# First products of a token pair from three experts instead of two, and a store moved from ScalarE's queue to SyncE's, in a chunked-scan and expert-merge kernel

## Chip, cores and metric

The kernel runs on one core of a Trainium2 chip. The metric is the device time of one execution in microseconds (us), the median of several runs. TensorE is the engine for matmuls (PE in the profile), VectorE is DVE, ScalarE is ACT, GpSimd is POOL, SyncE is SP.

## What is computed

Two parts follow each other. The first is a chunked state-space scan (Mamba-2 style) over 4 sequences, 8 heads, 768 positions, head size 32, state size 16. The second sends each of the 4 x 768 = 3072 tokens, now 256 wide, through 4 experts with 1024 hidden features each and adds the results by the token's domain probabilities:

```python
for c in range(nc):                      # chunks of a sequence
    L = np.exp(cum[:, :, :, None] - cum[:, :, None, :]) * causal
    y_intra = ((C @ B^T) * L) @ x        # inside the chunk
    y_inter = (C @ state) * np.exp(cum)  # from the chunks before
    state = decay_full * state + sum over j of (B x) * decay_from_j
...
p = domain_probs / (domain_probs.sum(-1, keepdims=True) + 1e-09)
for e in range(4):
    out += p[:, e:e+1] * (np.maximum(x @ w1[e], 0.0) @ w2[e])
```

All arithmetic is float32.

## The kernel before

**Tokens and weights.** Positions are worked on in 24 chunks of 128 tokens; two chunks make a pair of 256 tokens. The pairs are grouped into five blocks (`ORDER`, line 327): three blocks of two pairs (scheme `B`) and two of three pairs (scheme `H`). The experts' features are cut into 16 feature blocks `fb` of 256, four per expert (`EPB`, line 363). For a feature block `w1` and `w2` are 256 KB each.

**Products with sums.** The matmuls with `w1` and `w2` are not taken one by one: scheme `B` takes two feature blocks (a "two") and two pairs together and needs 7 products in place of 8, scheme `H` takes three and three and needs 15. Most products work on sums of weight halves (line 957) and sums of token halves (`token_sums`, lines 966 to 980, buffers `Y`). A product is two matmul instructions in the code (`product`, line 862, recorded at line 866) and four in the profile. In scheme `B` the products numbered 1 and 2 need neither kind of sum and only the first pair's tokens. `twos_begun` (line 1006) takes these two for one two: product 1, a copy of the bank by ScalarE (`snap`, line 873, recorded at 875), product 2 into the same bank, and then the gate: VectorE applies the ReLU and the probability (`gated`, line 898, recorded at 901). The rest of the two follows later in `twos_first` (line 1015), where ScalarE puts the copy back into a bank (`seed`, line 878, recorded at 880). The products with `w2` are gathered by `second` (line 1150); each `house` of results is copied out by ScalarE (1143, 1146).

**Scan side.** For a chunk, `fetch` (line 736) loads tokens (`xb`), decays spread over partitions (`ab`, line 434, from the stored table `acut_d`) and from the fifth chunk on the decays by head (`ah`, line 440, from the stored table `ac_d`). `decays` (line 750) has VectorE's scans (`LT`, line 490; `dec`, line 772), a small product on GpSimd (500) and ScalarE's masks (`ctm`, line 466). `scores` (line 779) is a matmul (473) and four masks on VectorE (`MT`, line 790); `outputs` (line 798) the matmuls that give the tokens (506, 812) and their copies by ScalarE (827, 516).

**Order.** Lines 383 to 692 are written in order by hand and treat the first two chunks. Line 691 stores the probabilities (`p_d`, from which the gate tables `gate` are loaded at line 854), line 692 stores `ac_d` by a DMA that ScalarE issues. Everything after is recorded as `Work` and ordered by `Plan.run` (line 182): it carries a clock for each engine with estimated costs, TensorE's order is fixed by the list `line`, and every other engine takes the ready work with the earliest due time. `KEEP` (used at 163) holds buffers back from work that is not urgent; `NEAR`, `WORTH` and `FIRST` (lines 232 to 237) let VectorE wait briefly for work that is more urgent than what is ready. So constants and TensorE's order decide the order on VectorE, ScalarE, GpSimd and in SyncE's queue, in which nearly all DMAs are issued. DMAs share eight completion counters, so an issue also waits until the DMA that had its counter eight places before has landed.

**The part at issue.** Lines 1286 to 1310 begin the planned part: four twos (feature blocks 0 to 7, two experts) get operands and `twos_begun`; their eight first products are put around `scores([2, 3])` and `outputs([2, 3])` (five ahead of the scores, `SCORED`, three behind), and then come the four products with `w2` that need nothing else (`second(0, ..., [(1, 2)])`). The loop from line 1340 goes through the units: for the first block unit 0 has feature blocks 0 to 3, unit 1 has 4 to 7 and so on. Lines 1344 and 1345 load a unit's weights one unit ahead. `EARLY` gives the units in which stored sums for scheme `H` are prepared, and `PAIRS_AT` the places in a unit's product list where the next block's chunks have their scores (`s`) and outputs (`o`).

Of the kernel before, what the change touches and what calls it, by code (L numbers as in the profile page):

```python
# [18 lines left out]
HOP = 0.06  # L19
D512, D256 = .60, .34  # L20
LANDING = 2.2
KEEP = 5
NV, NW = 33, 28
SLACK, BACK, YIELD = 0.0, 3.0, 0.0
EARLY = 3, 4, 5, 5, 6, 7, 8, 9, 10, 11
SOFT = 1
ROUND = 0, 3, 2, 0, 4
RATE, MARGIN = 330.0, 2.0
AFTER = 1
HOLD = 6.0  # L30
NEAR, WORTH, FIRST = .3, 3.0, 25.0
WAIT = .15
LANES, ISSUE = 8, .48
URGENT = {}
SCORED = 5
EASY = 40.0
HELD = ("x", "w"), (5, 8), (0, 7)
APART = (0, 7),
# [2 lines left out]
LATE = (13, 2), (6, 9), (11, 4), (10, 12), (3,), (1, 14), ("x", "w"), (5, 8), (0, 7)  # L41

PAIRS_AT = {
    (0, 2): ((1, 12, "s0"), (2, 5, "s1"), (2, 22, "o01")),
    (4, 2): ((0, 1, "s0"), (2, 1, "s1"), (2, 14, "o01")),
    (4, 3): ((0, 1, "s0"), (0, 14, "o0"), (1, 1, "s1"), (2, 1, "s2"), (2, 14, "o12")),
    (6, 3): ((0, 1, "s0"), (0, 14, "o0"), (2, 1, "s1"), (3, 1, "s2"), (3, 14, "o12")),
# [28 lines left out]
class Plan:  # L76
# [65 lines left out]
    def homed(self, w, at):  # L142

        taken, when = {}, at
        for v in w.touched:
# [14 lines left out]
            if v.kind == "bank" and len(self.spare["bank"]) <= sum(  # L160
                    x.home is None and x.place < v.place for x in self.banks):
                return None, None
            if v.kind == "V" and len(spare) <= KEEP and w.latest + self.late > at + 8:
                return None, None
# [172 lines left out]
def kernel(  # L337
# [10 lines left out]
    nc = tc.nc  # L348

    NCH, _, W = xbc.shape  # L350
# [12 lines left out]
    EPB = F // FB  # L363
# [24 lines left out]
    ac_d = tc.dram_tile([NCH, NH, P], FP32, name="ac_d")  # L388
# [137 lines left out]
    a_sb, a_cut = (homes["V"][-4][:NCH * NH // 2, i].rearrange("p (r s) -> p r s", r=2) for i in range(2))  # L526
# [62 lines left out]
    def store_decays(engine, d, sb):  # L589
        engine.dma_start(  # L590
            out=d.rearrange("c h s -> (c h) s").rearrange("(p r) s -> p r s", r=2), in_=sb)
# [97 lines left out]
        keep_state(1, A[1][:, t], y[:, P:])  # L689
    mask(2, ctm[0], xb[2])  # L690
    nc.sync.dma_start(out=p_d.rearrange("e c s -> c e s"), in_=p_sb)
    store_decays(nc.scalar, ac_d, a_sb)

# [1 line left out]
    line = []  # L697
# [308 lines left out]
    def twos_begun(k, fbs):  # L1006

        seq = []
        mul = opener(k, fbs, seq)
        b1 = mul(1)  # L1010
        s1 = snap(b1)
        mul(2, b1)
        return seq, s1, gated(b1, gate_of(k, fbs[0]), 0)
# [103 lines left out]
    def visit(k, house, terms, last=False, only=None):  # L1117

        seq = []
        terms = [t for t in terms if only in (None, t[0])]  # L1120
        held = kept.get((k, house))
        both = len({t[0] for t in terms}) == 2 or held is not None and held.both
        lo, to = 0, FB * (2 if both else 1)
        if only is not None:
            lo, to = FB * house.index(only), FB * house.index(only) + FB
        bank = seed(held, lo, to) if held is not None else value("bank", fills=both)
        begun = held is not None
        for which, w, view, x in terms:
            half = house.index(which)
            seq.append(plan.add({"PE": .863}, lambda e, half=half, view=view, x=x, begun=begun: product(  # L1130
                bank.t, half, view(), x.t, not begun), reads=[w, x], writes=[bank]))
            begun = True
        bank.both = both
        if last:
            kept[k, house if only is None else (only,)] = bank
            return seq
        v = kept[k, house] = value("V")
        v.both = both or len(house) == 2
        if not both and len(house) == 2:
            plan.add({"POOL": .4}, lambda e: nc.gpsimd.memset(  # L1140
                v.t[:, 1 - house.index(terms[0][0])], 0.0), part=[v])
        if both:
            act(.5, lambda e: nc.scalar.copy(out=flat(v), in_=bank.t), reads=[bank], writes=[v])  # L1143
        else:
            lo = FB * house.index(terms[0][0])
            act(.3, lambda e: nc.scalar.copy(  # L1146
                out=flat(v)[:, lo:lo + FB], in_=bank.t[:, lo:lo + FB]), reads=[bank], writes=[v])
        return seq

    def second(k, groups, houses, held=(), more=()):  # L1150

        seq = []
        for house in houses:
            terms = [
                (r, weights[k, fbs, 2][0][r][0], lambda r=r, fbs=fbs: weights[k, fbs, 2][1](r), T[r])
                for r in house for fbs, T in groups if r in T]
            terms += [t for t in more if t[0] in house]
            for only in reversed(house) if house in held and house in APART else (None,):
                if terms:
                    seq += visit(k, house, terms, house in held, only)  # L1160
        return seq
# [9 lines left out]
    def plain_terms(k, fbs, h, parts):  # L1171
        return [(blocks[k].scheme.plain[d, n], weights[k, fb, 2],
                 lambda fb=fb, d=d: w2_half(weights[k, fb, 2].t, d), h[fb, n])
                for d, n in parts for fb in fbs]
# [103 lines left out]
    def put(*seqs):  # L1278

        n = [len(s) for s in seqs]  # L1280
        keys = [((i + (.5 if len(seqs) == 1 else (j + .5) / len(seqs))) / n[j], j, i)
                for j, s in enumerate(seqs) for i in range(n[j])]
        return [seqs[j][i] for _, j, i in sorted(keys)]
# [3 lines left out]
    for l, at in ((1, 0), (2, 1)):  # L1287
        for i, fb in enumerate(range(0, 8 // l, 2)):
            loaded[fb, l] = plan.taken("W", fb + at, now + 1.0 + 0.6 * i)
    twos = [(fb, fb + 1) for fb in range(0, 8, 2)]  # L1290

    st[2]["a"] = [value("bank", fills=False) for _ in range(NQ)]
    fetch(3)
# [4 lines left out]
    for i in range(2):  # L1298
        tokens[0, i + 1] = yT[0, 0], lambda v, i=i: v.t[:, i]
    begun = {two: twos_begun(0, two) for two in twos}  # L1300
    firsts = [begun[twos[x + i]][0][j] for x in (0, 2) for j in range(2) for i in range(2)]
    decays(2)
    decays(3)
    line.extend(firsts[:SCORED])
    scores([2, 3])
    line.extend(firsts[SCORED:])
    outputs([2, 3])
    line.extend(second(0, [(two, {1: h}) for two, (_, _, h) in begun.items()], [(1, 2)]))
    for c in range(4):
        carry(c)  # L1310
    units, last_made = [], {}
# [28 lines left out]
    for u, (k, groups) in enumerate(units):  # L1340
        b = blocks[k]
        of_block = [v for v, (q, _) in enumerate(units) if q == k]
        i = u - of_block[0]
        if 1 < u + 1 < len(units):
            unit_weights(*units[u + 1])
        if i == 0 and k:
            token_sums(k)
        if groups is None:
            gates.pop((k, 0), None)
            seq, h = [], {}  # L1350
            for n in range(b.scheme.pairs):
                s, h[0, n] = plain_first(k, 0, n)
                seq += s
            plain = plain_terms(k, [0], h, b.scheme.plain)
        else:
            made = [threes_first(k, fbs) if b.scheme is H else twos_first(
                k, fbs, begun.get(fbs) if k == 0 else None) for fbs in groups]
            seq = put(*[s for s, _ in made])
            right = twos_right if b.scheme is B else threes_right
        merged = put(behind, seq) if behind else seq  # L1360
        ends.append(merged[-1])
        if ending is not None:
            leave(*ending, due=lambda n=u + AFTER: ends[min(n, len(ends) - 1)])
            ending = None
        for _ in range(EARLY.count(u)):
            operands("early", H, *early.pop(0), merged[0],
                     lambda n=u + SOFT: ends[min(n, len(ends) - 1)])
        if groups is None:
            behind = second(k, *held, HELD if k == len(blocks) - 1 else (), plain)
        else:  # L1370
            held = [(fbs, right(h)) for fbs, (_, h) in zip(groups, made)], b.scheme.houses
            for fbs, T in held[0]:
                if k == 0 and fbs in begun:
                    del T[1]
            plain_next = u + 1 < len(units) and units[u + 1][1] is None
            if plain_next:
                held = held[0], LATE
            behind = [] if plain_next else second(k, *held)
        if u == of_block[-1] and k < len(blocks) - 1:
            ending = k, result(k)  # L1380

        at = {}
        if k < len(blocks) - 1:
            for unit, x, what in PAIRS_AT[len(of_block) if k else 0, blocks[k + 1].scheme.pairs]:
                if unit != i:
                    continue
                cs = [blocks[k + 1].first + 2 * int(p) + j for p in what[1:] for j in range(2)]
                mark = len(line)
                if what[0] == "s":
                    for c in cs:  # L1390
                        fetch(c)
                        decays(c)
                    scores(cs)
                else:
                    outputs(cs)
                    for c in cs:
                        carry(c)
                at[x] = line[mark:]
                del line[mark:]
        for x, w in enumerate(merged):  # L1400
            line.extend(at.get(x, []))
            line.append(w)
# [54 lines left out]
```

## Time and profile before

| What | Value |
| --- | --- |
| time, median of 3 runs | 627.83 us (627.7, 627.83, 630.71) |
| the profiled execution's own time | 629.19 us |
| its span, first to last instruction | 627.2 us |
| granted TensorE clock in it | 0.998 of full speed |
| matmuls of line 866: instructions, busy | 2640, 428.4 + 211.7 us by tile |
| weight, token and table traffic | 127.45 MB, 203 GB/s in the mean |

The busy time of engines in stretches, and the share of time in which the DMA engines were busy:

| us | PE | DVE | ACT | POOL | DMA share | GB/s |
| --- | --- | --- | --- | --- | --- | --- |
| 0 to 10 | 10.00 | 7.37 | 4.09 | 6.57 | 0.61 | 190 |
| 10 to 20 | 8.26 | 6.24 | 5.09 | 1.51 | 0.76 | 261 |
| 20 to 30 | 9.95 | 10.00 | 6.13 | 0.42 | 0.95 | 317 |
| 30 to 40 | 8.83 | 10.00 | 4.65 | 0.56 | 1.03 | 381 |
| 40 to 50 | 10.00 | 9.85 | 4.59 | 3.10 | 0.82 | 258 |
| 50 to 60 | 10.00 | 8.72 | 2.73 | 6.58 | 1.00 | 323 |
| 60 to 80 | 20.00 | 20.00 | 8.29 | 12.55 | 0.72 | 242 |
| 80 to 100 | 20.00 | 19.85 | 12.27 | 11.41 | 0.76 | 252 |
| 100 to 150 | 50.00 | 47.15 | 19.34 | 22.16 | 0.64 | 211 |
| 150 to 627 | 471.43 | 390.49 | 207.40 | 98.47 | 0.59 | 188 |

In the profile's rows a tile's buffer number is left out: `bank` is an accumulation bank, `v` a token or result buffer, `w` a weight buffer, `Y` a sum of tokens. A row of the timeline gives start, length, engine, line, operation, what is written and read, the number of merged instructions, and in brackets the idle time of the engine before it and what ended that. ACTq and SPq are the queues of ScalarE and SyncE at a DMA issue. In a list of waits the numbers are total time, times, and the longest.

### The profile page before, as it was taken

How to read it: one execution, taken by the hardware profiler on the slowest of the kernel's cores; microseconds unless marked ns; L12 is line 12 of the kernel's file. 1: busy time of each engine (PE TensorE's matmuls, PEld its weight loads, DVE VectorE, ACT ScalarE, POOL GpSimd, SP SyncE). 2: the span in 40 equal slices, each digit the busy share in tenths (PEclk: the TensorE clock that was granted, in tenths of full speed). 3: DMA queues.
4: the chain of work that ended last, by engine and by line, in shares of the span. 5: the costliest groups of instructions: out<-in, count | busy, mean ns of one | idle time of the engine just before them, and what ended most of it. 6: DMA issues, size and time to landing. Idle time of an engine off the chain costs nothing.

```text
span 627.2 us, 10263 instructions
## 1 busy us (share of the span) xinstructions
PE 617.3 (98%) x3427; PEld 525.9 (84%) x3427; DVE 529.6 (84%) x886; ACT 274.6 (44%) x580; POOL 163.3 (26%) x201
## 2 busy tenths in 40 slices
PE   8999999999999999999999999999999999999997
PEld 4778888888888888888788888888888888888886
DVE  7899999996878798869689989959786977869684
ACT  4533463433355344235534345445444335454441
POOL 4016656630385664333441000100020000000000
PEclk9999999999999999999999999999999999999999
DMA  7798768663699978389999737636222329743001
GB/s 251 263 357 302 237 206 286 212 206 108 210 353 372 301 236 299 98 261 345 336 357 299 242 71 249 194 96 200 61 93 68 82 50 299 225 142 110 1 1 51
DMA packets 112629, 127.45 MB, mean 203 GB/s; under 512 B 28981, under 2 KB 78145, under 8 KB 112577
## 3 DMA queue, kind: packets, MB, share of 16 engines
q1 hardware_dynamic: 112308, 126.64, 62.1%
q8 instruction: 27, 0.44, 0.3%
q14 instruction: 26, 0.20, 0.1%
q10 hardware_dynamic: 268, 0.16, 0.1%
HBM read 101.87 MB, written 24.89 MB: 202 GB/s over the span
## 4 chain that ended last, share of the span: by engine, by line
PE 83%; DVE 8%; DMA 3%; SPq 3%; issue 2%; ACT 1%; POOL 0%; ACTq 0%; DVEq 0%; POOLq 0%
PE bank L866 79%; DVE v L893 3%; SPq L1250 2%; DMA w<-in_w_dram 2%; DVE v L901 2%; PE bank L506 1%; PE bank L473 1%; DMA xb<-in_xbc_dram 1%; DVE w L957 1%; DVE MT L790 1%; DVE LT L490 1%; PE bank L812 1%; DVE v L1195 0%; ACT v L875 0%; ACT A L516 0%
## 5 line engine op out<-in xcount | busy, mean ns | idle before, releaser
L866 PE MATMUL bank<-v,w 128*128 128x256 f32 x1816 | 428.4, 380 | 2.0 <-ACT v L875 1.7
L866 PEld LDWEIGHTS bank<-v,w 128*128 128x128 f32 x1816 | 343.1, 190 | 53.9 <-issue 2.8
L866 PE MATMUL bank<-Y,w 128*128 128x256 f32 x824 | 211.7, 380 | 2.9 <-ACT v L875 1.3
L893 DVE TENSOR_TENSOR v<-v,v 128x512 f32<-128x512 f32 x269 | 188.8, 735 | 26.1 <-ACT v L875 24.7
L866 PEld LDWEIGHTS bank<-Y,w 128*128 128x128 f32 x824 | 155.6, 190 | 27.5 <-ACT v L875 2.7
L880 ACT COPY bank<-v 128x512 f32<-128x512 f32 (+1 forms) x200 | 112.2, 571 | 81.1 <-DVE v L893 47.0
L901 DVE SCALAR_TENSOR_TENSOR v<-bank,gate 128x512 f32<-128x512 f32 x172 | 116.6, 683 | 31.6 <-PE bank L866 26.9
L875 ACT COPY v<-bank 128x512 f32<-128x512 f32 x112 | 65.3, 584 | 101.5 <-PE bank L866 101.2
L957 POOL TENSOR_TENSOR w<-w,w 128x256 f32<-128x256 f32 x105 | 91.6, 894 | 40.2 <-PE bank L866 18.4
L1143 ACT COPY v<-bank 128x512 f32<-128x512 f32 x105 | 61.4, 584 | 90.4 <-PE bank L866 88.0
L893 POOL TENSOR_TENSOR v<-v,v 128x512 f32<-128x512 f32 x11 | 18.4, 1669 | 281.4 <-DVE v L893 142.6
L490 DVE TENSOR_TENSOR_SCAN LT<-ab,ident 128x512 f32<-128x512 f32 x42 | 53.4, 1290 | 2.1 <-DMA ab<-acut_d 2.1
L893 DVE TENSOR_TENSOR v<-bank,v 128x512 f32<-128x512 f32 x40 | 27.4, 685 | 6.7 <-PE bank L866 6.2
L790 DVE TENSOR_TENSOR MT<-bank,LT 128x512 f32<-128x512 f32 x44 | 27.3, 680 | 1.2 <-PE bank L473 1.2
L1195 DVE TENSOR_TENSOR v<-v,v 128x256 f32<-128x256 f32 x54 | 21.8, 437 | 7.7 <-ACT v L1143 7.6
L500 POOL TENSOR_TENSOR MT<-xb,LT 128x64 f32<-128x64 f32 (+1 forms) x28 | 14.2, 514 | 48.5 <-DVE LT L490 25.6
L957 POOL TENSOR_TENSOR w<-w 128x256 f32<-128x256 f32 x14 | 16.1, 1155 | 37.4 <-DMA w<-in_w_dram 18.9
L1146 ACT COPY v<-bank 128x256 f32<-128x256 f32 x23 | 8.6, 372 | 35.7 <-PE bank L866 35.5
L775 POOL TENSOR_TENSOR cts<-ctm,dec 128x256 f32<-128x256 f32 x20 | 16.2, 816 | 26.7 <-ACT ctm L466 19.7
L466 ACT ACTIVATE ctm<-xb,tmask 128x128 f32<-128x128 f32 x48 | 16.5, 396 | 13.3 <-DMA xb<-in_xbc_dram 11.9
L1042 DVE TENSOR_TENSOR bank<-bank,v 128x512 f32<-128x512 f32 x24 | 16.4, 687 | 3.5 <-PE bank L866 3.5
L957 DVE TENSOR_TENSOR w<-w,w 128x256 f32<-128x256 f32 x33 | 15.4, 503 | 0.0
(72 smaller groups left out, 204.5 us busy)
## 6 DMA issues: line engine op xcount, KB each, us to landing
w<-w_d SPq DMA_DIRECT2D x138, 256.0 KB
w<-in_w_dram SPq DMA_DIRECT2D x126, 256.0 KB
w_d<-w SPq DMA_DIRECT2D x82, 256.0 KB
ab<-acut_d SPq DMA_DIRECT2D x21, 512.0 KB
w<-in_w_dram SPq DMA_DIRECT2D x42, 128.0 KB
gate<-p_d SPq DMA_DIRECT2D x10, 384.0 KB
xb<-in_xbc_dram SPq DMA_DIRECT2D x17, 192.0 KB
gate<-p_d SPq DMA_DIRECT2D x11, 256.0 KB
```

Source lines behind the costliest of these rows:

```text
L466: nc.scalar.mul(ctm[:, t], xb[:, OCT:OCT + P], tmask[:, t:t + 1])
L490: nc.vector.tensor_tensor_scan(out=LT.rearrange("p h s -> p (h s)")[:, lo:lo + w], data0=src, data1=ident.rearrange("p h s -> p (h s)")[:, ...
L790: nc.vector.tensor_mul(s["MT"].t[:, js, h, 0:P], g, s["LT"].t[:, js, h])
L866: nc.tensor.matmul(out=o, lhsT=w[:, j], rhs=x if half is None else x[:, j], start=(start and j == 0), stop=(j == 1), skip_group_check=True)
L875: act(.5, lambda e: nc.scalar.copy(out=flat(v), in_=bank.t), reads=[bank], writes=[v])
L880: act(.54 if to - lo > FB else .32, lambda e: nc.scalar.copy(out=bank.t[:, lo:to], in_=flat(v)[:, lo:to]), reads=[v], writes=[bank])
L893: plan.add(engines, lambda e: (on(e).tensor_add if sign > 0 else on(e).tensor_sub)(flat(v), whole(x), whole(y)), reads=[x, y], writes=[v], ...
L901: dve(D512, lambda e: nc.vector.scalar_tensor_tensor(out=h.t, in0=whole(x).rearrange("p (j m) -> p j m", j=JJ), scalar=0.0, in1=g.t[:, 2 * ...
L957: plan.add({"POOL": .72} if due else B256, lambda e, r=r, x=x, y=y, sign=sign: (on(e).tensor_add if sign > 0 else on(e).tensor_sub)(view(r ...
L1042: dve(D512, lambda e: nc.vector.tensor_sub(b5.t, b5.t, flat(t)), reads=[t], writes=[b5])
L1143: act(.5, lambda e: nc.scalar.copy(out=flat(v), in_=bank.t), reads=[bank], writes=[v])
L1195: plan.add(engines, lambda e: (on(e).tensor_add if sign > 0 else on(e).tensor_sub)(o[1](), x[1](), y[1]()), reads=[v for v in vs if v is n ...
```

## The change

It takes the first products of the first pair ahead for six twos (feature blocks 0 to 11, three experts, `AHEAD`) instead of four. The four added first products stand behind `outputs([2, 3])`, two added products with `w2` follow with the others, and units 0, 1 and 2 of the first block no longer load their weights a unit ahead, since they are all named at the start. The store of `ac_d` goes into SyncE's queue. The numbers that steer the plan change too: `KEEP`, `WORTH`, `SCORED`, `EARLY` and the places of the second block's chunks. `MIXED` is false, so its branch is not taken; in the last hunk two pieces of scan work at the same place would both be kept.

```diff
-KEEP = 5
+KEEP = 4
-EARLY = 3, 4, 5, 5, 6, 7, 8, 9, 10, 11
+EARLY = 2, 3, 4, 5, 6, 7, 8, 9, 10, 11
-NEAR, WORTH, FIRST = .3, 3.0, 25.0
+NEAR, WORTH, FIRST = .3, 1.0, 25.0
-SCORED = 5
+SCORED = 4
+AHEAD = 3
+MIXED = False
...
-    (0, 2): ((1, 12, "s0"), (2, 5, "s1"), (2, 22, "o01")),
+    (0, 2): ((1, 9, "s0"), (2, 1, "s1"), (2, 18, "o01")),
...
-    store_decays(nc.scalar, ac_d, a_sb)
+    store_decays(nc.sync, ac_d, a_sb)
...
-    twos = [(fb, fb + 1) for fb in range(0, 8, 2)]
+    twos = [(fb, fb + 1) for fb in range(0, AHEAD * EPB, 2)]
...
-    firsts = [begun[twos[x + i]][0][j] for x in (0, 2) for j in range(2) for i in range(2)]
+    firsts = [begun[twos[x + i]][0][j] for x in range(0, len(twos), 2) for j in range(2) for i in range(2)]
...
     line.extend(firsts[:SCORED])
     scores([2, 3])
-    line.extend(firsts[SCORED:])
+    line.extend(firsts[SCORED:8])
     outputs([2, 3])
-    line.extend(second(0, [(two, {1: h}) for two, (_, _, h) in begun.items()], [(1, 2)]))
+    line.extend(put(firsts[8:], second(0, [(two, {1: begun[two][2]}) for two in twos], [(1, 2)])) if MIXED else [
+        *firsts[8:], *second(0, [(two, {1: begun[two][2]}) for two in twos], [(1, 2)])])
...
-        if 1 < u + 1 < len(units):
+        if AHEAD <= u + 1 < len(units):
             unit_weights(*units[u + 1])
...
-                at[x] = line[mark:]
+                at.setdefault(x, []).extend(line[mark:])
```

## The prediction

> **What bounds the kernel now.** I read the engine rows of the page first:
>
> ```profile
> PE 617.3 (98%) x3427; PEld 525.9 (84%) x3427; DVE 529.6 (84%) x886; ACT 274.6 (44%) x580; POOL 163.3 (26%) x201
> ```
>
> TensorE (PE) is busy 617.3 of 627.2 us, so only its waits can be won. The Trainium skill (Trainium Kernel Development and Optimization, Performance Expectations) says that matmul busy time is a bad measure of the distance to the limit, and that the busy share of the weight loads is a good one. By that rule 16% of the span, 100 us, would be open. The rows speak against it here: where nothing waits, x4 matmuls of L866 (one product) start every 0.86 us (45.54, 46.41, 47.27 in the timeline), 216 ns apiece, whatever the weight loads leave free. The change keeps the number of products, so I count only what exceeds 216 ns a matmul. The waits of TensorE in the first 60 us come next (total, times, longest):
>
> ```profile
> PE bank L866 <- ACT v L875: 1.7, 1, 1.7
> PE bank L866 <- ACT bank L880: 0.9, 1, 0.9
> PE bank L866 <- DVE v L901: 0.2, 1, 0.2
> ```
>
> Over the whole span the list adds 1.3 us for L875 and 0.7 us for L790; these lie near 309, 378 and 406 us. The timeline of TensorE (start, length, what, idle before) places the early ones:
>
> ```profile
> 12.68 1.99 PE L866 MATMUL bank<-v,w 128*128 128x256 f32 x8
> 16.42 2.86 PE L866 MATMUL bank<-v,w 128*128 128x256 f32 x12 [1.75 <-ACT v L875]
> ...
> 24.75 3.72 PE L866 MATMUL bank<-v,w 128*128 128x256 f32 x16
> 28.31 5.93 PE L866 MATMUL bank<-Y,w 128*128 128x256 f32 x24
> 35.10 2.33 PE L866 MATMUL bank<-Y,w 128*128 128x256 f32 x8 [0.86 <-ACT bank L880]
> 37.67 2.86 PE L866 MATMUL bank<-v,w 128*128 128x256 f32 x12 [0.24 <-DVE v L901]
> ```
>
> From row to row I subtract count x 0.216: 16.42 - 12.68 - 1.73 = 2.01 us lost; 35.10 - 28.31 - 5.18 = 1.61; 37.67 - 35.10 - 1.73 = 0.84. Together 4.5 us; all else before 60 us loses 0.1 to 0.3 at changes of shape. The first loss is explained by the timelines of ScalarE, VectorE and SyncE's queue:
>
> ```profile
> 13.16 0.69 ACT L466 ACTIVATE ctm<-xb,tmask 128x128 f32<-128x128 f32 x2
> 14.76 0.35 ACTq L590 DMA_DIRECT2D ac_d<-v  x1
> 15.21 0.69 ACT L466 ACTIVATE ctm<-xb,tmask 128x128 f32<-128x128 f32 x2 [1.36 <-DMA w<-in_w_dram]
> 15.81 1.05 ACT L875 COPY v<-bank 128x512 f32<-128x512 f32 x2
> ```
>
> ```profile
> 13.30 2.39 DVE L490 TENSOR_TENSOR_SCAN LT<-bank,ident 128x256 f32<-128x256 f32 x4
> 17.67 0.69 DVE L901 SCALAR_TENSOR_TENSOR v<-bank,gate 128x512 f32<-128x512 f32 x1 [1.98 <-PE bank L866]
> 18.28 2.33 DVE L490 TENSOR_TENSOR_SCAN LT<-ab,ident 128x512 f32<-128x512 f32 x2
> ```
>
> ```profile
> 12.17 0.51 SPq L448 DMA_DIRECT2D w<-in_w_dram  x1
> 16.51 0.34 SPq L854 DMA_DIRECT2D gate<-p_d  x1
> 16.90 0.43 SPq L448 DMA_DIRECT2D w<-in_w_dram  x1
> ```
>
> ScalarE stands at its DMA issue (L590) until a weight load lands; the masks of chunk 3 and the first copies (L875) queue behind it, and TensorE waits for a copy. SyncE issues nothing from 12.68 to 16.51. VectorE idles until 17.67 and is then full until 49 us, where the losses at 35 and 37 lie.
>
> **The store on SyncE's queue.** It leaves ScalarE (0.35 us of issue, and the wait before it) and joins SyncE's queue behind L691. A rule of the Trainium skill (same page, Key Constraints) speaks against a gain: queues share the DMA engines, and issuing from several engines only saves sequencer time. By the rule the move is worth ScalarE's 0.35 us and costs SyncE as much. By the row the issue also holds ScalarE from 13.76 (13.16 plus 0.60, the spacing of 15.21 and 15.81) to 15.21: 1.45 us. I take the row. Chunk 3's tokens must have landed: issued at 7.70, and the weight load issued at 8.88 landed 5.86 us later in the chain view, so by the same delay 13.6; at the latest with that load, 14.73. So masks 13.76, copies 14.36 to 14.94, TensorE again at 14.98: 1.44 us won; at the late bound 0.5. On SyncE 96 KB and one issue (about 0.35 us) come ahead of one weight load, inside the empty stretch 12.68 to 16.51, which hides them; without it 0.35 us on every later load.
>
> **Six products moved forward.** The two twos of the third expert bring four first products (two each) and two second ones: 6 x 0.864 = 5.18 us of TensorE go from unit 2 to before unit 0. The built order has 1722 TensorE instructions in both kernels, so nothing is added. SCORED 4 puts the scores one product earlier, which swaps neighbours. Walk of TensorE after: four products to 16.71 (12.68 + 3.46 + 0.57 of wait), scores 1.08 to 17.8, four products to 21.24. VectorE now scans chunk 3 when its decays have landed, not after the gate of the first product: at the latest 16.5, when SyncE's L854 had seen the younger transfer of L691. 16.5 + 2.33 + 2.48 (four masks L790) = 21.3, so outputs run 21.3 to 22.9 instead of 23.15. Next the four new products: their second halves wait for two L875 copies, which stand behind the copies of the outputs and four L516 pieces each on ScalarE (24.39 to 26.5 before, 1.9 earlier now): the last starts at 25.8 where TensorE is ready at 25.5. Loss 0.3 to 0.4 plus 0.1 to start again. Six second products then end at 31.8, where the first product with sums starts. Before it was 28.31; 28.31 + 5.18 = 33.5, so 1.7 us are won by there.
>
> **Weights behind them.** Unit 2's two loads of w1 and two of w2 (1 MB) and a gate table (256 KB) now go ahead of the operands of unit 0's sums. 1.25 MB at 317 GB/s (windows row 20 to 30 us, DMA share 0.95) is 4 us; SyncE's empty stretch takes one load that before left at 16.90. So sums' operands land some 3.3 us later, and TensorE asks for them 3.5 us later: hidden, with little to spare. VectorE's two more gates (0.6 each) come earlier, not anew.
>
> **The losses at 35 and 37.** They came from gates (L901) behind weight sums on VectorE, with each bank refilled only after its gate. In the new order the next product refills another bank, so the loss at 35 goes. But VectorE's order now puts a scan half (1.2 us, L490) between two gates of unit 0; a product waits for the second: 38.7 + 1.2 + 0.6 = 40.5 against 39.7, so 0.8 us stay late, and the gate before adds 0.1. The small waits between 28 and 34 (1.61 less 0.86 and its restart, some 0.6) follow the same alternation of two banks, and I keep 0.5.
>
> **Sum.** Lost before 4.5. Lost after: 0.57 and 0.1 at 14.4; 0.45 at 25; 0.5 in the sums' products; 0.9 to 1.1 at 38 to 40: 2.6. Won 1.9; VectorE says the same another way: full from 17.67, it starts its backlog 1.2 to 1.6 us earlier. Further on (KEEP, EARLY, WORTH, the places of the pairs) the order changes until about row 315 of TensorE's 1722 and is then the same; no loss shows there before. VectorE's last 364 instructions and ScalarE's last 234 keep their order, so I keep the losses at 378 and 406. At 309 ScalarE's mask waits for tokens; one mask now stands three copies earlier in that order, worth between -0.8 and +1.4 us; the nearest row is the old wait, so 0. I take 2.0 won. The profiled execution took 629.19 for a span of 627.2; it would take 627.2, and the median, 1.36 below that execution, goes from 627.83 to 625.8.
>
> **Rivals.**
> - All waits close: the scan does not fall between the gates, and the wait at 309 goes. 1.9 + 1.0 + 1.3 = 4.2 won: 623.6. For it: the list of waits has no other entry of weight. Against: the built order of VectorE shows the scan there.
> - VectorE is the limit from 20 to 49 us (10.00, 10.00 and 9.85 busy in the windows), and its two early gates and one more combine (TensorE's first sums wait in its line) eat the start: 0.5 won, 627.3.
> - Slower, by the DMA engines: they are full from 20 to 60 us (share 0.95, 1.03, 0.82, 1.00), and 12.8 MB go through in 40 us there (317, 381, 258, 323 GB/s). All later operands now follow 1.25 MB more. The first sum of unit 2 comes at 53.4 us when I carry the walk on, its load lands near 46.5: 7 us of slack. If the stretch runs at 258 GB/s throughout, 12.8 MB take 9.6 us more: 2.6 us late, VectorE stands at that sum in order with the gates behind it and TensorE behind the gates: 2.0 won less 2.6, 628.4. At the 242 GB/s of the row 60 to 80 it is 12.9 us, 5.9 late, 631.7. It decides from about 245 GB/s down. Against: the same transfers, mostly in the same sizes, made 320 in the mean, and the row at 40 to 50 has a share of only 0.82, so it is not the engines' limit.
> - The store moves but ScalarE then waits for tokens until 14.73: 0.9 less, 626.7, inside the likeliest range.
>
> **Chances.** Likeliest case 0.50 (625.8, own range 624.7 to 627.0), all waits close 0.24, VectorE 0.13, slower 0.13. Within 0.5% (3.1 us, about what a measurement of this kernel can tell from no change) lie the likeliest and VectorE: 0.62 after a little of the likeliest goes faster; faster 0.25, slower 0.13. The range 623.4 to 629.3 takes in the 258 GB/s of the slower case, leaves out the rest of it and the far edge of the best: under 2 in 10.
>
> **What would show it.** The copies L875 start near 14.4 and TensorE's row near 15.0; no ACTq row for ac_d; the first product with Y near 31.8; its 0.86 wait on L880 gone, a wait on L901 near 39; VectorE idle for under 1 us near 16. A wait of TensorE on DVE w L957 or of VectorE on DMA w in 22 to 32 us would show the slower rival; a new wait past 80 us would make the sum wrong.

## The result and the profile after

| | before | after |
| --- | --- | --- |
| median of 20 runs each | 628.44 us | 626.26 us |
| ratio after to before, 95% interval | | 0.9963 [0.9948, 0.9977] |
| the profiled execution, its span | 629.19, 627.2 us | 626.43, 624.6 us |
| granted clock in it | 0.998 | 1.000 |

One of the 20 runs after was disturbed (2292.82 us) and is left out of the ratio. The change wins 2.2 us by the medians, 0.37%. The forecast said 2.0 us and "within 0.5%", and both hold. The two profiles differ by 2.6 us of span, 0.4 us more than the medians, so a part of what follows belongs to these two executions and not to the change. How that sum comes about differs from the forecast, and the traces and four experiments show where.

The first part of the page after gives the engines' busy time:

```profile
PE 617.5 (99%) x3427; PEld 525.4 (84%) x3427; DVE 534.4 (86%) x888; ACT 273.5 (44%) x580; POOL 170.5 (27%) x199
```

TensorE has the same 3427 instructions and the same busy time (617.5 for 617.3). What has gone is waiting. Line numbers after are two or three higher: products 868, copies 877, seeds 882, gates 903, masks of the scores 792, scan 492, ScalarE's masks 468, the store 592.

The timeline of TensorE after, over the stretch shown of before:

```profile
12.49 1.99 PE L868 MATMUL bank<-v,w 128*128 128x256 f32 x8
14.84 1.99 PE L868 MATMUL bank<-v,w 128*128 128x256 f32 x8 [0.36 <-ACT v L877]
...
17.84 3.80 PE L868 MATMUL bank<-v,w 128*128 128x256 f32 x16
21.80 1.69 PE L508 MATMUL bank<-MT,xb 128*32 128x144 f32 x32 [0.15 <-DVE MT L792]
23.41 3.06 PE L868 MATMUL bank<-v,w 128*128 128x256 f32 x12
26.71 6.31 PE L868 MATMUL bank<-v,w 128*128 128x256 f32 x28 [0.24 <-ACT v L877]
32.86 7.55 PE L868 MATMUL bank<-Y,w 128*128 128x256 f32 x32
40.40 1.13 PE L868 MATMUL bank<-v,w 128*128 128x256 f32 x4
42.11 1.99 PE L868 MATMUL bank<-v,w 128*128 128x256 f32 x8 [0.58 <-DVE v L903]
```

Read it as before: start to start, less 216 ns a matmul. 14.84 - 12.49 - 1.73 = 0.62 lost at the first copies (2.01 before). 21.80 - 17.84 - 3.46 = 0.50 ahead of the outputs (0.27 before, at 20.29). 26.71 - 23.41 - 2.59 = 0.71 at the added products. 0.10 up to 32.86, then 0.63 in the sums' products to 40.40, then 42.11 - 40.40 - 0.86 = 0.85 at a gate. Together 3.4 us. Before, by the same count, the three losses make 4.5 and the two changes of shape (0.27, and 0.10 at 24.75) another 0.4: 4.8 us. That is 1.4 us won, and the first product starts 0.19 earlier in this profile. Matmul by matmul, the kernel after leads by 1.54 us at 112 us, which fits.

ScalarE's timeline shows the cure at its root:

```profile
12.96 1.36 ACT L468 ACTIVATE ctm<-xb,tmask 128x128 f32<-128x128 f32 x4
14.23 1.04 ACT L877 COPY v<-bank 128x512 f32<-128x512 f32 x2
```

All four masks run in one piece and the copies follow at once. No ACTq row stands between. The store is now in SyncE's queue:

```profile
12.43 0.51 SPq L592 DMA_DIRECT2D ac_d<-v  x1
12.99 0.98 SPq L450 DMA_DIRECT2D w<-in_w_dram  x2
17.39 0.34 SPq L856 DMA_DIRECT2D gate<-p_d  x1
```

It takes 0.51 us of a queue that issues nothing from 13.97 to 17.39. VectorE's timeline has the two places where the forecast was to be tested (the second part is from around 40 us):

```profile
17.32 2.34 DVE L492 TENSOR_TENSOR_SCAN LT<-ab,ident 128x512 f32<-128x512 f32 x2 [1.82 <-DMA ab<-acut_d]
19.77 2.48 DVE L792 TENSOR_TENSOR MT<-bank,LT 128x512 f32<-128x512 f32 x4
...
39.06 1.28 DVE L903 SCALAR_TENSOR_TENSOR v<-bank,gate 128x512 f32<-128x512 f32 x2
40.26 1.22 DVE L492 TENSOR_TENSOR_SCAN LT<-ab,ident 128x512 f32<-128x512 f32 x1
41.39 0.67 DVE L903 SCALAR_TENSOR_TENSOR v<-bank,gate 128x512 f32<-128x512 f32 x1
```

The scan of chunk 3 waits for its decays (`ab`) until 17.32, and the masks of the scores end at 22.2; the outputs start on the first ones at 21.80. At 40.26 a scan half stands between two gates, and TensorE's product at 42.11 waits for the second of them.

Further on, the lead changes at four places. A new loss at 113 us takes 0.29 of it, a loss of before at 292 that is gone adds 0.20, so that it is 1.45 at 306 us (times of the kernel after). From 307.87 on it is 2.56, and a second new loss at 345 takes 0.27. Another 0.25 of the span's 2.6 lies behind the last matmul. The big step is near 309. ScalarE's and TensorE's rows there, before and then after:

```profile
309.22 0.69 ACT L466 ACTIVATE ctm<-xb,tmask 128x128 f32<-128x128 f32 x2 [2.79 <-DMA xb<-in_xbc_dram]
309.82 0.56 ACT L875 COPY v<-bank 128x512 f32<-128x512 f32 x1
310.43 1.13 PE L866 MATMUL bank<-Y,w 128*128 128x256 f32 x4 [1.28 <-ACT v L875]
```

```profile
306.65 0.69 ACT L468 ACTIVATE ctm<-xb,tmask 128x128 f32<-128x128 f32 x2 [1.83 <-DMA xb<-in_xbc_dram]
307.25 0.56 ACT L877 COPY v<-bank 128x512 f32<-128x512 f32 x1
307.87 1.13 PE L868 MATMUL bank<-Y,w 128*128 128x256 f32 x4 [0.16 <-ACT v L877]
```

A mask waits for its chunk's tokens, and a copy that TensorE needs stands behind it in ScalarE's order. The mask is that of chunk 20, whose scores run at 373 us after and at 375 before, so it is not what TensorE wants here; it merely stands in front. TensorE waits 0.16 us for the copy where it waited 1.28.

### The profile page after: what moved, and what is told of

Read it like the earlier page. It is cut to its first block, busy times and chain, and to the rows that moved or that the text cites. A ratio compares the mean times of both kernels' runs of the same rounds, so it can differ in the third digit from the quotient of the medians.

```text
span 624.6 us, 10268 instructions
## 1 busy us (share of the span) xinstructions
PE 617.5 (99%) x3427; PEld 525.4 (84%) x3427; DVE 534.4 (86%) x888; ACT 273.5 (44%) x580; POOL 170.5 (27%) x199
## 4 chain that ended last, share of the span: by engine, by line
PE 84%; DMA 6%; DVE 5%; issue 1%; SPq 1%; POOL 1%; ACT 1%; DVEq 0%; POOLq 0%; ACTq 0%
PE bank L868 81%; DMA ab<-acut_d 2%; DMA xb<-in_xbc_dram 2%; DVE v L903 2%; DVE v L895 2%; PE bank L508 1%; PE bank L475 1%; SPq L1252 1%; DMA acut_d<-v 1%; DVE LT L492 1%; DMA w_d<-w 1%; POOL w L959 1%; PE bank L814 1%; DVE MT L792 0%; DMA v<-in_a_dram 0%
## 5 line engine op out<-in xcount | busy, mean ns | idle before, releaser
L895 DVE TENSOR_TENSOR v<-v,v 128x512 f32<-128x512 f32 x270 | 194.4, 751 | 21.9 <-ACT v L877 20.1
L959 POOL TENSOR_TENSOR w<-w,w 128x256 f32<-128x256 f32 x103 | 98.8, 979 | 51.8 <-PE bank L868 32.3
L895 POOL TENSOR_TENSOR v<-v,v 128x512 f32<-128x512 f32 x10 | 16.0, 1598 | 263.2 <-DVE v L895 208.8
L492 DVE TENSOR_TENSOR_SCAN LT<-ab,ident 128x512 f32<-128x512 f32 x42 | 54.9, 1323 | 4.3 <-DMA ab<-acut_d 4.3
L502 POOL TENSOR_TENSOR MT<-xb,LT 128x64 f32<-128x64 f32 (+1 forms) x28 | 16.3, 589 | 63.1 <-DVE LT L492 44.0
L468 ACT ACTIVATE ctm<-xb,tmask 128x128 f32<-128x128 f32 x48 | 16.5, 395 | 18.0 <-DMA xb<-in_xbc_dram 18.0
L1044 DVE TENSOR_TENSOR bank<-bank,v 128x512 f32<-128x512 f32 x24 | 16.5, 689 | 4.5 <-PE bank L868 4.5
L959 DVE TENSOR_TENSOR w<-w,w 128x256 f32<-128x256 f32 x35 | 16.5, 506 | 0.0
```

The costliest lines, as they stand in the source:

```text
L468: nc.scalar.mul(ctm[:, t], xb[:, OCT:OCT + P], tmask[:, t:t + 1])
L492: nc.vector.tensor_tensor_scan(out=LT.rearrange("p h s -> p (h s)")[:, lo:lo + w], data0=src, data1=ident.rearrange("p h s -> p (h s)")[:, ...
L895: plan.add(engines, lambda e: (on(e).tensor_add if sign > 0 else on(e).tensor_sub)(flat(v), whole(x), whole(y)), reads=[x, y], writes=[v], ...
L959: plan.add({"POOL": .72} if due else B256, lambda e, r=r, x=x, y=y, sign=sign: (on(e).tensor_add if sign > 0 else on(e).tensor_sub)(view(r ...
```

## The experiments

All four ran on one chip, 12 runs each, beside 35 runs of the kernel before (629.52 us there). The kernel after was not run among them; where an experiment is set beside it, each is taken as its ratio to the kernel before.

**The store alone.** The kernel before with one line changed:

```diff
-    store_decays(nc.scalar, ac_d, a_sb)
+    store_decays(nc.sync, ac_d, a_sb)
```

> The kernel before with the store of the decays on SyncE's queue and nothing else; every other engine keeps its order. My theory: ScalarE's first copies start near 14.4 us, TensorE loses 0.6 us there instead of 2.0, VectorE starts its full stretch 1.4 to 1.6 us earlier, and with it the losses at 28 to 38 move and stay as long; 1.4 us won, ratio 0.998, spans near 625.8. Rival, that VectorE's full stretch sets the pace and the six moved products are what fills it: the 1.4 us turn up again as longer waits of TensorE between 28 and 40 us, at most 0.4 us won, ratio 0.9995. Both leave the wait at 309 us at 1.3 to 1.5 us.

Measured: 628.1 us, 0.9978 [0.9962, 0.9993], so 1.4 us won. TensorE's timeline:

```profile
13.02 1.99 PE L866 MATMUL bank<-v,w 128*128 128x256 f32 x8
15.29 2.86 PE L866 MATMUL bank<-v,w 128*128 128x256 f32 x12 [0.28 <-ACT v L875]
```

15.29 - 13.02 - 1.73 = 0.54 us lost instead of 2.01: 1.47 won at the place itself. The losses of before at 35 and 37 are all still there, with the same waits (0.86 on L880, 0.24 on L901), at 33.95 and 36.53. They don't grow when TensorE comes earlier, as the rival had it. The move by itself is worth what it wins at the first copies, as expected. In this one profile the lead, 1.14 us up to 288, is lost again by 309 at several waits under 0.6 us, and 0.79 comes back at 310, where TensorE waits 0.48 us and not the 1.3 to 1.5 that were expected; by the medians the gain stays.

**The store back on ScalarE.** The kernel after with the reverse edit, all else as after:

```diff
-    store_decays(nc.sync, ac_d, a_sb)
+    store_decays(nc.scalar, ac_d, a_sb)
```

> The changed kernel with the store put back on ScalarE's queue; only ScalarE's and SyncE's orders change. My theory: ScalarE stands at the issue again, TensorE loses about 2.0 us at 14.4, scans and outputs come about 1.4 us later, and the kernel ends 1.2 to 1.4 us later than the changed one: of the 2.3 us won over before 1.0 is left, ratio 0.9985. Rival: VectorE waits for chunk 3's decays until 17.3 us anyway, so that what TensorE loses at 14.4 is hidden by that wait, and 0.3 us or less are lost: ratio 0.997.

Measured: 629.26 us, 1.0000 [0.9984, 1.0016]. The whole gain is gone; that is more than the theory (0.9985) and its rival (0.997) had expected. Against the kernel after's 0.9963 the store costs about 2.3 us here (0.0037 x 628.44), where in the old order it cost 1.4. ScalarE's timeline, then TensorE's, then the row of 18 to 22 us from the busy time in windows (PE, PEld, DVE, ACT, POOL, then granted clock, DMA share, GB/s):

```profile
13.41 0.69 ACT L468 ACTIVATE ctm<-xb,tmask 128x128 f32<-128x128 f32 x2
16.39 0.35 ACTq L592 DMA_DIRECT2D ac_d<-v  x1
16.85 0.69 ACT L468 ACTIVATE ctm<-xb,tmask 128x128 f32<-128x128 f32 x2 [2.74 <-DMA ab<-acut_d]
17.45 1.05 ACT L877 COPY v<-bank 128x512 f32<-128x512 f32 x2
```

```profile
12.94 1.99 PE L868 MATMUL bank<-v,w 128*128 128x256 f32 x8
18.06 3.64 PE L868 MATMUL bank<-v,w 128*128 128x256 f32 x8 [3.13 <-ACT v L877]
```

```profile
18.00:22.00 4.00, 3.94 (x16) 2.75 (x20) 0.83 (x1) 0.49 (x2) 0.41 (x1) 0.57 0.70 198
```

Two things make the same store dearer. The issue is held longer: it is now released by the landing of the decays `ab` and not, as before, by that of a weight load, and comes at 16.39 instead of 14.76 (why is told under "The store" below), so TensorE starts again 18.06 - 12.94 - 1.73 = 3.39 us late instead of 2.01. And then TensorE runs at half clock: the row of 18.06 has 8 matmuls in 3.64 us, where 8 take 1.99 elsewhere in the same table, so 1.65 us more; the window's clock is 0.57, and 1.00 in the same window of before and after. By the medians of this kernel's own runs: 6 of 12 have a mean clock of 0.997 or less and a median of 630.13 us, the 6 others have 1.000 and 628.81. The profiled execution is one of the first six. So the half clock comes in some runs and costs about 1.3 us when it does; in the other runs the store still costs.

**The products alone.** As the last kernel, and with four of the plan's constants back at their old values (the places of the second block's chunks stay as after, because one of the old places lies beyond the end of the shortened unit 2):

```diff
-KEEP = 4
+KEEP = 5
-EARLY = 2, 3, 4, 5, 6, 7, 8, 9, 10, 11
+EARLY = 3, 4, 5, 5, 6, 7, 8, 9, 10, 11
-NEAR, WORTH, FIRST = .3, 1.0, 25.0
+NEAR, WORTH, FIRST = .3, 3.0, 25.0
-SCORED = 4
+SCORED = 5
-    store_decays(nc.sync, ac_d, a_sb)
+    store_decays(nc.scalar, ac_d, a_sb)
```

> The six products moved forward, with the store on ScalarE's queue and KEEP, EARLY, WORTH and SCORED as before; the places of the second block's chunks stay as changed, since unit 2 is now shorter than the old place. My theory: the loss of 2.0 at 14.4 stays, those at 35 and 37 shrink to about 1 us, the wait at 309 may be either; 0.5 to 1.0 us won, ratio 0.9988. Rival, the products are worth nothing by themselves since VectorE is full: 0.0, ratio 1.000. Rival, they are the whole gain: 2.0 us, 0.9965.

Measured: 631.83 us, 1.0025 [1.0007, 1.0044]. Six products moved forward without the store's move make the kernel 1.6 us slower (2.3 by the two medians), where theory and rivals had all expected a gain or nothing. The same two things are seen, in ScalarE's and TensorE's timelines and the row of 18 to 22 us:

```profile
16.00 0.69 ACT L468 ACTIVATE ctm<-xb,tmask 128x128 f32<-128x128 f32 x2 [2.06 <-DMA ab<-acut_d]
17.22 4.54 PE L868 MATMUL bank<-v,w 128*128 128x256 f32 x12 [2.45 <-ACT v L877]
18.00:22.00 4.00, 4.00 (x14) 3.00 (x16) 0.88 (x2) 0.20 (x1) 0.41 (x1) 0.58 0.94 287
```

The mask waits for `ab` behind the issue, TensorE for the copy behind the mask, and the clock falls to half. Here 11 of the 12 runs have a mean clock of 0.997 or less, and the twelfth, at 1.000, took 628.76 us. So its slowness beside the kernel before goes with the half clock, but one run with full clock is too few to put a figure on the rest.

**The old constants, with the store moved.** The last kernel's edit without its last two lines:

```diff
-KEEP = 4
+KEEP = 5
-EARLY = 2, 3, 4, 5, 6, 7, 8, 9, 10, 11
+EARLY = 3, 4, 5, 5, 6, 7, 8, 9, 10, 11
-NEAR, WORTH, FIRST = .3, 1.0, 25.0
+NEAR, WORTH, FIRST = .3, 3.0, 25.0
-SCORED = 4
+SCORED = 5
```

> The changed kernel with KEEP 5, EARLY, WORTH 3 and SCORED 5 as before; products and store as changed. My theory: the early gain of about 1.5 us does not hang on these numbers, and only the 1.1 us at 309 us come from the order that they make: ratio 0.9975, with a wait of TensorE near 309 of 1 us or more. Rival, the steering numbers are needed for the early gain: ratio 0.9990 or more, with new waits of TensorE on VectorE's gates before 60 us.

Measured: 628.71 us, 0.9982 [0.9965, 0.9999]. That is no better than the store alone (0.9978), so no gain of the six products with the old constants shows. The ratio lies between the theory's 0.9975 and the rival's 0.9990 and decides for neither; the wait near 309 that the theory wanted is not there, and a new wait before 60 us, as the rival wanted, is, though on masks behind a gate. TensorE loses most in its first row of outputs:

```profile
22.87 1.69 PE L508 MATMUL bank<-MT,xb 128*32 128x144 f32 x32 [0.96 <-DVE MT L792]
```

and VectorE's timeline says why:

```profile
18.01 2.34 DVE L492 TENSOR_TENSOR_SCAN LT<-ab,ident 128x512 f32<-128x512 f32 x2 [2.53 <-DMA ab<-acut_d]
20.27 0.67 DVE L903 SCALAR_TENSOR_TENSOR v<-bank,gate 128x512 f32<-128x512 f32 x1
20.85 2.47 DVE L792 TENSOR_TENSOR MT<-bank,LT 128x512 f32<-128x512 f32 x4
```

The decays land 0.69 us later than in the kernel after (they are asked for at 11.38 and 11.10), and a gate, 0.58 us, stands ahead of the masks that the outputs need; in the kernel after the masks come first. That is 1.27 us, of which 1.07 reach the outputs (22.87 for 21.80), since VectorE in the kernel after pauses 0.2 us between scans and masks. The first cause is this profile's DMA timing, only the second is the edit. Between this kernel and the one after lie 0.0019, 1.2 us; the intervals overlap, so a part of the constants is possible but not secured, and which of the four does it was not tried singly.

## Why the prediction held, step by step

**The store: right in place, size and reason.** Forecast 1.44 us at the first copies, TensorE again at 14.98. Measured 2.01 - 0.62 = 1.39 in the kernel after (TensorE again at 14.84), 1.47 in the kernel with the store alone, and 1.4 us of that kernel's median (of which some may be half clock spared, see the last section). The late bound of 0.5 and the rival with ScalarE waiting for tokens did not occur here: the four masks have no wait among them. (With the old constants there was one of 0.24 us.)

Why the issue was held, and why it no longer is, stands in the semaphores of the traces, the completion counters of the DMAs. DMAs use eight of them by turns to report that they have landed, and an issue waits until the last user of its semaphore has. In the kernel before the store got that of the weight load issued at 8.88, in the two kernels with the store back that of `ab`: four issues back each time, not eight. On SyncE it got that of the store of `acut_d`, issued at 6.38 and landed at 11.03, and waited for nothing. So the move took away the wait itself and did not only shift it to another queue. A store on ScalarE with a free semaphore was not tried; an estimate from the rows is little more than its 0.35 us of issue.

The rule set against it (issuing from several engines saves only sequencer time, the Trainium skill's "Trainium Kernel Development and Optimization", Key Constraints) would have given 0.35. It leaves out that an issue which waits holds up the compute behind it on the same engine, and here that was the price. The rule on busy shares, weighed in the forecast, would have left 100 us open; this change takes away waits alone and does not test it.

**The six products: too good by about 1 us at 32 us.** Forecast was 31.8 for the first product with `Y`; it starts at 32.86. The step that failed within it is "at the latest 16.5" for the landing of chunk 3's decays. It took SyncE's release of L854 before as a bound, but that was a bound for the old set of transfers.

After, the decays landed at 17.20. They were issued 0.26 us later (11.10 for 10.84), which the change has no part in: up to there the transfers are the same in all six profiles, and that issue comes between 10.31 and 11.38. The rest is the way from issue to landing. It took 5.16 us before, 5.04 with the store alone, 5.04 and 5.22 in the two kernels with the store back, where one more 256 KB weight load follows; but 6.10 in the kernel after and 6.51 with the old constants, where the 96 KB store and the added load both follow. So neither alone delays the decays, as far as these profiles tell, and both together do, by about 1 us in two profiles of two. It is one late part: of the 16 that a landing reports, 15 were in by 16.17 and 16.43, and the last came 1.0 and 1.5 us behind them; why that one, no trace tells.

The store's ride on SyncE was hidden from the queue but not from the DMA engines, and the scan started at 17.32, 0.8 us after the bound. So VectorE idled 1.82 us there, where under 1 us was the sign named. The outputs came at 21.80, not 21.3, and the loss at the added products was 0.71 where 0.45 was forecast.

**The weights: right.** No wait of TensorE for weight sums and none of VectorE for a weight load appears from 22 to 60 us. The windows after have 324, 384 and 296 GB/s in 20 to 30, 30 to 40 and 40 to 50 us, well over the 245 at which the slower rival would have decided.

**The losses at 35 and 37: right, with the scan half where it was put.** The 0.86 wait on the seed (L880) is gone, and the store alone left it in place, so it went with the products and the plan. 0.63 is lost in the sums' products (0.5 forecast) and 0.85 behind the scan half (0.9 to 1.1 forecast), at 42.1 rather than 40.5. The rival in which all waits close needed this one gone.

**The sum: right by luck, since errors cancel.** The forecast's two counts of the early part differ. Its walk has 1.7 us won by the first product with `Y`, and its losses at 35 to 40 us (1.4 to 1.6 for 2.45) 0.9 to 1.0 more, 2.6 in all; its sum books 1.9, because on the side of before it leaves out three changes of shape ahead of `Y` (0.20, 0.27 and 0.10) and on the side of after counts some. By the walk the miss is 1.2, by the sum 0.5: early, 1.9 was forecast and 1.4 won; near 309, 0 was taken between -0.8 and +1.4, and 1.1 came.

The reason given there, a mask three copies earlier in ScalarE's order, doesn't explain it alone: a mask still waits (1.83 us), but the tokens land sooner, their load being issued at 300.05 us instead of 302.10. In the five other profiles that mask starts between 308.90 and 309.55 whatever the edit, only in the profile after as early as 306.65. The three with the moved products have no wait of TensorE there, but TensorE is 2.0 to 2.6 us behind the kernel before when it comes to it, so they can't tell a cure from lateness. The stretch of 280 to 310 us is full of transfers, and single profiles differ there by about 1 us, so how much of the 1.1 belongs to the change and how much to this execution stays open. The sign that would have spoken against the sum, a new wait past 80 us, came twice and small (0.29 at 113, 0.27 at 345). What can be said from medians is smaller: 2.2 us in all, 1.4 of it from the store alone, some 0.9 from the rest together with it (0.9978 to 0.9963, whose intervals overlap).

**VectorE as the limit: no.** It is idle 0.61 us in 30 to 40 us, waiting for TensorE (0.50 of it at 37.85), in a stretch where it had been full before.

**What the forecast missed.** It added the parts as if each had a price of its own. The experiments speak for a bond between the two: the store on ScalarE costs 1.4 us in the old order and 2.3 in the new, and the products with their constants are worth 0.9 with the store moved and nothing (1.0000 within 0.0016) without. By the times this is not secured: the difference of 0.9 us has an interval of some 1.7 us to either side, an estimate from the three intervals. What the traces do show is the longer hold (3.39 for 2.01 us lost) and the half clock behind it. One experiment not made would be the shortest way to the rest: the two gates put ahead of the scan half at 40 us, worth up to 0.85 by the timeline.

## What to carry to other kernels

A DMA issue in a compute engine's queue costs its wait, not its 0.35 us: look at what releases it and what compute stands behind it, and put it in a queue that has nothing urgent behind it. The edit can also change which older DMA it waits for, so look again afterwards. Its bytes still go through the same DMA engines, so a landing time read from the old profile is no bound for the new one. Before adding the gains of several edits, ask which one sets the wait that the others lengthen or shorten.

## What the runs showed of the hardware

- **Half clock behind a short wait.** TensorE ran 8 matmuls at about 427 ns instead of 216 behind idle times of 2.45 and 3.13 us, with a granted clock of 0.57 to 0.58 over 4 us. In finer windows it is 0.50 for 3.41 us in both profiles, from 17.93 and 18.24 on, which is 0.71 and 0.18 us after TensorE had started again. Behind 1.75 us (the kernel before) the clock stayed 1.00 in its profile. The Trainium skill ("TensorE: Matmul & The Clock Gate", Part 1: The HAM clock gate) puts the fall to half rate behind at least one idle window of about 3.4 us and says that this window runs freely, so that the point varies. The runs here have it after less than that: in one of them TensorE was busy for 0.98 us of the 3.43 us ahead of the fall. It came in 6 of 12 and 11 of 12 runs if the mean clock is the sign, so a wait of 2.5 us must be priced with some 1.3 to 1.7 us of half clock as well. No run with a filled gap was made, so that the gap causes it rests on the order of events alone.
- **The mean clock as a sign across runs.** 3.41 us at half rate take 0.0027 off the mean over 627 us, so 0.997 is the value to look for. Of the 35 runs of the kernel before, 8 have 0.997 or less and a median of 630.57 us; the 27 others have 628.89. With the store off ScalarE such runs are rare: none of 12, none of 12, and 1 of 19. This fits a half clock that the 2.0 us gap of before brings on in some runs, but no profile of that kernel caught one, so its cause stays open there. (Its one profile has 0.998 from a low clock at the very end, 0.71 over the last 3 us, where it costs nothing.) If it is that, part of the store's 1.4 us is spared half clock: beside 628.89 the kernel with the store alone, 628.1, is 0.8 us faster.
- **An issue waits for another queue's DMA.** ScalarE's store was held by a weight load and by the decays' load, both issued by SyncE, until they had landed, since it was to use their semaphore next. Which load it is changes with the order of issues: the semaphore was free at 14.73 us in the old order and at 16.37 in the new, and the store issued 0.03 and 0.02 us later.
